# A one-token decode block on one core: the loads move from SyncE's queue to GpSimd's, one packet for each engine's share

## The chip, the cores and the metric

One core of a Trainium2 chip runs the kernel. The metric is the device time of one execution in microseconds (us). Three runs of the kernel before gave 1275.4, 1275.68 and 1275.88 us, a median of 1275.68 us.

## What is computed

The reference, cut to what matters. The key and value caches are bf16 and hold 8 heads of 65536 rows of 256 elements: 268 MB each, read once. Everything else is small.

```
B, Sq, D = 1, 1, 448;  Hq, Hkv, Sk, Dh = 16, 8, 65536, 256
xn = layernorm(A_x)
q = (xn @ A_wq) as 16 heads of 256
scores = q . k_cache * 256**-0.5          # two query heads share a key head
o = softmax(scores) . v_cache             # per head
attn = o.reshape(1, 4096) @ A_wo
g = silu(xn @ B_w_gate); u = xn @ B_w_up; y = (g * u) @ B_w_down
ffn = xn + y * sigmoid(xn @ B_w_r)
out = A_x + attn + ffn
```

## The kernel before

**Tiling.** The 65536 rows of a head are spread over 128 partitions, 512 rows to a partition. A load is a quarter of a head: 128 rows of 512 bytes on each partition, so 64 KB in one piece from each partition, 8192 KB in all. There are 32 such loads of keys (K0 to K31 here) and 32 of values (V0 to V31). In the code U is 4 (quarters), NU is 32, NT is 28, so V28 is `("v", NT)` and V31 is `("v", NT + 3)`. SBUF has three slots of one load each (`ring`): even K in the first, odd K in the second, V0 to V27 in the third. K0 to K4 are loaded in two halves of 4096 KB each, and V31 in five parts of 64, 32, 16, 8 and 8 rows.

**Engines.** For a K load, TensorE transposes the keys (`ps_t`), VectorE and ScalarE copy them out of PSUM (`kt_all`), TensorE multiplies them with the query (`ps_q`), and the scores are gathered in `S_sb`. After four K loads of a head comes the softmax's exponential, and then its four V loads go through `ps_o`. All matrix products of TensorE are recorded under one line, L413; all DMA issues under L914.

**Queues.** Each engine's instructions are put into a list (`prog`) by Python and emitted in that order; a wait at the head of a list holds all that stands behind it. `item` (L241) puts waits and DMA issues on SyncE's list (SP). The order is: `k_first` (the first 16 of the 64 rows of K0's first half, 1024 KB, L288), `wq` (the query's weights, 3584 KB, into the third slot, L289), the rest of K0's first half, K0's second half, K1's halves, then K2 and K3 and V0 and so on, each with a wait for its slot: `FREE` (a K load is transposed), `FREEH` (its first half is), `VFREE` (a V load is multiplied). Near the end stand V28, then the weights `wg` (gate and up, two DMAs), `wd` (down, and x again), `wo` (most of the output weights, 2912 KB), then V29, V30, and V31, which waits for `SUM`, then `wx` and `wo_end` (the rest of the output weights). The last DMA, the output, is on SyncE's list too.

**The other DMAs.** ScalarE's queue issues four small ones: x and w_r at the start (`w0`, L387), and two hops near the end (`hop`, L678). Hop 0 writes `o_row`, the attention output of the first seven heads, 14 rows of 512 bytes, to `o_flat` in HBM; hop 1, which waits for hop 0, reads it back as `oT_h`, 56 bytes on each of 128 partitions. In `ending` (L801) TensorE's order is: V28, the feed-forward products, `ATTN` (L682, the products of `oT_h` with `wo`), then V29, V30, V31. VectorE adds up `SUM` (L828 to L833) after `ATTN`. V31's slot holds `wo`, `oT_h` is read by `ATTN`, and so V31 waits for `SUM`.

**GpSimd** runs `pool_setup` (L315: constants) at the start and nothing afterwards. VectorE's setup begins with a wait for one of these (`z_m1p`, L348), and its layer norm waits for both loads of `w0` (L355).

Of the kernel before, what the change touches and what calls it, by code (L numbers as in the profile page):

```python
# [23 lines left out]
def bass_parallel_sum__gqa_block_cached__moe_arch_mod__decode_kernel(  # L24
# [149 lines left out]
    sems = {}  # L174
# [20 lines left out]
    prog = {e: [] for e in engines}  # L195
    here = [("S", 0)]
# [7 lines left out]
    def put(e, kind, key, fn, sem):  # L204
        if ghost[0] and e == "pe":
            prog[e].append(("g" + kind, lab(e), key, fn, sem))
        elif not ghost[0]:
            prog[e].append((kind, lab(e), key, fn, sem))

    def W(e, *key):  # L210
        put(e, "w", key, None, None)
# [3 lines left out]
    def O(e, key, fn, sem=None, n=1):  # L215
        key = key if isinstance(key, tuple) else (key,)
        if not ghost[0]:
            weight[key] = n
        put(e, "o", key, fn, sem or e)

    def alias(e, *key, sem=None):
        put(e, "a", key, None, sem or e)
# [15 lines left out]
    semtot = {}  # L238
    fed = {}

    def item(key, parts, need=()):  # L241
        for n in need:
            W("sp", *n)
        for ap, src, sem in parts:
            semtot[sem] = semtot.get(sem, 0) + 16
            items[key] = (sem, semtot[sem])
            prog["sp"].append(("d", here[0], ("DMA", key, len(prog["sp"])), (ap, src), sem))

    def rows_src(kd, u, o, J):
        src = A_k_cache if kd == "k" else A_v_cache  # L250
# [64 lines left out]
    def pool_setup():  # L315
        v = nc.gpsimd
        O("pool", "z_identf", lambda it: v.memset(ident_f[:, :], 0.0))
        O("pool", "ones", lambda it: v.memset(ones_f[:, :], 1.0))
        O("pool", "z_sel", lambda it: v.memset(sel_bf[:, :, :], 0.0))
        O("pool", "z_sel2", lambda it: v.memset(sel2_bf[:, :, :], 0.0))  # L320
        O("pool", "z_m1p", lambda it: v.memset(m1p[:, :, :], 0.0))
        O("pool", "z_zero", lambda it: v.memset(zero_bf[:, :], 0.0))
        W("pool", "z_identf")
        O("pool", "identf", lambda it: v.affine_select(
            out=ident_f[:, :], in_=ident_f[:, :], compare_op=ALU.not_equal, fill=1.0,
            base=0, pattern=[[-1, P]], channel_multiplier=1))
        W("pool", "identf")
        O("pool", "identbf", lambda it: v.tensor_copy(out=ident_bf[:, :], in_=ident_f[:, :]))
        W("pool", "identbf")
        for m in range(NG):  # L330
            for i in range(rep):
                O("pool", ("sel", m, i), lambda it, m=m, i=i: v.tensor_copy(
                    out=sel_bf[:, m, i:i + 1], in_=ident_bf[:, 32 * m + i:32 * m + i + 1]))
        for g in range(NG):
            for i in range(rep):
                for n2 in range(2):
                    if g > 0:
                        W("pool", "sel2", g - 1, i, n2)
                    r = 32 * g + n2 * rep + i
                    O("pool", ("sel2", g, i, n2), lambda it, r=r, i=i, n2=n2: v.tensor_tensor(  # L340
                        out=sel2_bf[:, n2, i:i + 1], in0=sel2_bf[:, n2, i:i + 1], in1=ident_bf[:, r:r + 1], op=ALU.add))
        alias("pool", "CONST")
        O("pool", "z_q", lambda it: v.memset(q_cur[:, :, :], 0.0))
        O("pool", "KZ", lambda it: v.memset(kt_all[:, :], 0.0))

    def dve_setup():
        v = nc.vector
        W("dve", "z_m1p")  # L348
        O("dve", "XEZ", lambda it: v.memset(xe_row[:, :, :, :], 0.0), "sc")
        O("dve", "PSQ_ZERO", lambda it: v.memset(ps_q[:, :], 0.0), "ev0")  # L350
        O("dve", "PSO_ZERO", lambda it: v.memset(ps_o[:, :], 0.0), "ev1")
        O("dve", "s2z0", lambda it: v.memset(s2[0][:, :], 0.0), "ev2")
        O("dve", "pssz", lambda it: v.memset(ps_s[:, :], 0.0))
        O("dve", "S2Z", lambda it: v.memset(s2[1][:, :], 0.0))
        W("dve", "DMA", "w0")  # L355
        O("dve", "xf", lambda it: v.tensor_copy(out=x_f, in_=x_row))
        W("dve", "xf")
        O("dve", "mean", lambda it: v.tensor_reduce(out=stat[0:1, 0:1], in_=x_f, axis=AX.X, op=ALU.add))
        W("dve", "mean")
        O("dve", "negmean", lambda it: v.tensor_scalar(out=stat[0:1, 7:8], in0=stat[0:1, 0:1], scalar1=-1.0 / D, scalar2=None,  # L360
                                                       op0=ALU.mult))
        W("dve", "negmean")
        O("dve", "xc", lambda it: v.tensor_scalar(out=xc_f, in0=x_f, scalar1=stat[0:1, 7:8], scalar2=None, op0=ALU.add))
        W("dve", "xc")
        O("dve", "sumsq", lambda it: v.tensor_tensor_reduce(out=xn_f, in0=xc_f, in1=xc_f, scale=1.0, scalar=0.0,
                                                            op0=ALU.mult, op1=ALU.add, accum_out=stat[0:1, 1:2]))
        W("dve", "sumsq")
        O("dve", "VPE", lambda it: v.tensor_scalar(out=stat[0:1, 2:3], in0=stat[0:1, 1:2], scalar1=1.0 / D, scalar2=EPS,
                                                   op0=ALU.mult, op1=ALU.add))
        W("dve", "SQRT")  # L370
        O("dve", "rstd", lambda it: v.reciprocal(out=stat[0:1, 4:5], in_=stat[0:1, 3:4]))
        W("dve", "rstd")
        O("dve", "xn", lambda it: v.tensor_scalar(out=xn_f, in0=xc_f, scalar1=stat[0:1, 4:5], scalar2=None, op0=ALU.mult))
        W("dve", "xn")
        O("dve", "XNBF", lambda it: v.tensor_copy(out=xn_bf, in_=xn_f))
        W("dve", "XNBF")
        W("dve", "XEZ")
        xv = xn_bf.rearrange("o (u s) -> o u s", s=RP)
        for t in range(2):
            e_ = xe_row[0:1, t, :, :].rearrange("o r (u t) -> o r u t", t=2)[:, :, :, t]  # L380
            O("dve", ("xe", t), lambda it, e_=e_, t=t: v.tensor_copy(
                out=e_, in_=xv[:, :, t * (NE - 1):t * (NE - 1) + NE].rearrange("o u r -> o r u")))
        alias("dve", "XE")
        O("dve", "R", lambda it: v.tensor_tensor_reduce(out=x_f, in0=xn_bf, in1=wr_row, scale=1.0, scalar=0.0,
                                                        op0=ALU.mult, op1=ALU.add, accum_out=stat[0:1, 5:6]))

    def act_setup():  # L387
        a = nc.scalar
        for k, (d, s) in enumerate([(x_row, A_x[0]), (wr_row, B_w_r.rearrange("(o n) -> o n", o=1))]):
            prog["act"].append(("d", here[0], ("w0", k), (d, s), "w0"))  # L390
        items["w0"] = ("w0", 32)
        W("act", "VPE")
        O("act", "SQRT", lambda it: a.activation(out=stat[0:1, 3:4], in_=stat[0:1, 2:3], func=ACTF.Sqrt), "evq")
        W("act", "R")
        O("act", "SIG", lambda it: a.activation(out=stat[0:1, 6:7], in_=stat[0:1, 5:6], func=ACTF.Sigmoid), "ev3")
        W("dve", "XNT")
        x = ps_m[0:P, C_XNT:C_XNT + 2 * NE].rearrange("p (t r) -> p r t", t=2)
        y = xnT_sb[:, 0:2 * NE].rearrange("p (r t) -> p r t", t=2)
        z = xnT_sb[:, 2 * NE:4 * NE - 2].rearrange("p (r t) -> p r t", t=2)
        O("dve", "xnt0", lambda it: nc.vector.tensor_copy(out=y, in_=x), "exp")  # L400
        O("dve", "xnt1", lambda it: nc.vector.tensor_copy(out=z[:, :, 0], in_=x[:, 1:NE, 1]))
        O("dve", "XNTSB", lambda it: nc.vector.tensor_copy(out=z[:, :, 1], in_=x[:, 0:NE - 1, 0]))
        W("dve", "QT")
        O("dve", "QTSB", lambda it: nc.vector.tensor_scalar(
            out=qT_sb[:, :, :], in0=ps_m[0:P, C_Q:C_Q + NH * Hq].rearrange("p (q f) -> p f q", f=NH), scalar1=inv_sqrt_dh, scalar2=None, op0=ALU.mult), "pc", 2)
        W("act", "QTSB")
        W("act", "S2Z")
# [393 lines left out]
    def ending():  # L801
# [66 lines left out]
        W("sp", "RESULT", 1)  # L868
        prog["sp"].append(("d", here[0], ("OUT", 0), (out[0], res_bf), "out"))

    pool_setup()
    dve_setup()
    act_setup()
    pe_setup()
# [23 lines left out]
    def emit(e, tail=False):  # L898
        eng = engines[e]
        waited = {}  # L900
        pool = []
# [8 lines left out]
        def do(kind, key, fn, sem, it):  # L910
            if kind == "o":
                fn(it).then_inc(sems[sem], weight[key])
            elif kind == "d":
                eng.dma_start(fn[0], fn[1]).then_inc(sems[sem], 16)  # L914

        def fit(vals, execs, inner):

# [165 lines left out]
        while k < len(entries):  # L1083
            kind, lab, key, fn, sem = entries[k]
# [60 lines left out]
```

## Time and profile before

| | |
|---|---|
| median of three runs | 1275.68 us |
| profiled execution, its own time | 1275.51 us |
| its span, first to last instruction | 1274.2 us |
| TensorE busy | 75% |
| VectorE, ScalarE, GpSimd busy | 45%, 34%, 1% |
| read from HBM | 549 MB, 431 GB/s over the span |

The profiled execution's time is 1.3 us above its span. It is within 0.2 us of the median. Busy shares are shares of the span; a DMA engine counts as busy while one of its packets is in work, and there are 16 such engines.

### The profile page before, as it was taken

The page shows a single profiled execution, that of the slowest core. Times are in us where ns is not written, and L with a number is a line of the kernel's source. Part 1 is how long each engine was busy: PE and PEld are TensorE (multiplying, and loading weights), DVE is VectorE, ACT ScalarE, POOL GpSimd, SP SyncE. Part 2 cuts the span into 40 slices and gives each one's busy share as a digit, 9 for nine tenths or more (in the row PEclk, how much of TensorE's full clock was granted, in tenths as well). Part 3 has the DMA queues.
Part 4 walks back from the last instruction along what each step waited for, and adds up shares of the span by engine and source line. Part 5 has one row for each costly group of instructions (what it writes and reads, how often), then busy time and mean ns, then how long its engine had stood idle before and what let it go on. Part 6 is the DMA issues. An engine that isn't in the chain of part 4 may idle for free.

```text
span 1274.2 us, 23495 instructions
## 1 busy us (share of the span) xinstructions
PE 957.2 (75%) x9729; PEld 624.0 (49%) x9729; DVE 572.1 (45%) x1078; ACT 436.9 (34%) x656; POOL 8.0 (1%) x38
## 2 busy tenths in 40 slices
PE   3899977778777679777778776787777687777854
PEld 3676554445544455444455444454444554444411
DVE  4666544345444455343454444453444544444310
ACT  2455433244332434223333243343333333323300
POOL 2000000000000000000000000000000000000000
PEclk9999988899888899887898888898888988888887
DMA  9999999999999999999999999999999999999998
GB/s 409 427 434 433 441 428 432 438 428 438 436 428 432 438 428 442 432 430 430 438 428 444 430 430 430 438 428 446 428 430 430 438 428 446 428 430 432 430 432 370
DMA packets 12273, 549.22 MB, mean 431 GB/s; under 512 B 1490, under 2 KB 2020, under 8 KB 2532
## 3 DMA queue, kind: packets, MB, share of 16 engines
q1 hardware_dynamic: 12084, 549.03, 99.8%
q8 instruction: 8, 0.13, 0.0%
q10 hardware_dynamic: 176, 0.02, 0.0%
q14 instruction: 5, 0.04, 0.0%
HBM read 549.04 MB, written 0.01 MB: 431 GB/s over the span
## 4 chain that ended last, share of the span: by engine, by line
DMA 76%; PE 19%; ACT 2%; issue 1%; DVE 1%; SPq 0%; ACTq 0%; DVEq 0%
DMA ring<-in_A_v_cache_dram 68%; PE ps_o L413 13%; DMA ring<-in_A_k_cache_dram 4%; PE ps_t L413 4%; DMA kt_all<-in_A_wo_dram 3%; PE ps_q L413 2%; ACT kt_all L474 2%; PE ps_m L413 1%; DVE kt_all L472 0%; ACT S_sb L555 0%; SPq L914 0%; PE ps_s L413 0%; DVE kt_all L718 0%; DVE m1p L525 0%; DVE S_sb L523 0%
## 5 line engine op out<-in xcount | busy, mean ns | idle before, releaser
L413 PE MATMUL ps_t<-ident_f,ring 128*128 128x128 f32 x4096 | 585.0, 284 | 78.1 <-DMA ring<-in_A_k_cache_dram 53.3
L472 DVE COPY kt_all<-ps_t 128x1024 bf16<-128x1024 bf16 x768 | 487.0, 685 | 285.4 <-PE ps_q L413 281.1
L413 PEld LDWEIGHTS ps_t<-ident_f,ring 128*128 128x128 f32 x4096 | 449.4, 143 | 230.0 <-issue 136.4
L474 ACT ACTIVATE kt_all<-ps_t 128x1024 bf16<-128x1024 bf16 x256 | 262.2, 1024 | 500.5 <-PE ps_q L413 500.4
L413 PE MATMUL ps_o<-ring,p_sb 128*4 128x512 bf16 x2044 | 180.7, 517 | 214.0 <-DMA ring<-in_A_v_cache_dram 209.6
L413 PEld LDWEIGHTS ps_o<-ring,p_sb 128*4 128x4 bf16 x2044 | 53.7, 103 | 303.8 <-issue 278.2
L413 PE MATMUL ps_q<-kt_all,q_cur 128*2 128x512 bf16 x2056 | 164.3, 396 | 0.4 <-DVE kt_all L472 0.3
L496 ACT ACTIVATE s<-ps_q 98x512 bf16<-98x512 f32 x257 | 151.8, 591 | 1.3 <-PE ps_q L413 1.3
L578 DVE RECIPROCAL rs<-ps_m 128x4 f32<-128x4 f32 x29 | 5.3, 183 | 279.0 <-PE ps_m L413 279.0
L565 ACT ACTIVATE p_sb<-S_sb 128x128 bf16<-128x128 bf16 x64 | 18.9, 307 | 282.4 <-PE ps_o L413 282.1
L413 PEld LDWEIGHTS ps_s<-sel_bf,s 128*128 128x128 bf16 x1032 | 64.5, 98 | 4.7 <-ACT s L496 1.3
L634 DVE CAST ob_sb<-ps_o 100x512 bf16<-100x512 f32 x29 | 20.1, 692 | 99.2 <-PE ps_o L413 99.2
L413 PE MATMUL ps_s<-sel_bf,s 128*128 128x8 bf16 x1032 | 63.6, 167 | 1.0 <-ACT s L496 1.0
L413 PEld LDWEIGHTS ps_q<-kt_all,q_cur 128*2 128x2 bf16 x2056 | 26.4, 79 | 44.0 <-issue 44.0
L413 PEld LDWEIGHTS ps_m<-rowsum,ones_f 128*128 128x128 f32 x58 | 12.5, 269 | 23.6 <-issue 23.6
L474 ACT ACT_TABLE_LOAD x7 | 9.0, 1283 | 20.6 <-PE ps_q L413 20.6
L525 DVE TENSOR_REDUCE m1p<-S_sb (+1 forms) x33 | 13.9, 422 | 4.4
L413 PE MATMUL ps_m<-rowsum,ones_f 128*128 128x4 f32 x58 | 15.1, 330 | 0.0
L555 ACT ACTIVATE S_sb<-S_sb,negmax 128x512 bf16<-128x512 bf16 x16 | 13.2, 852 | 3.3 <-DVE negmax L549 3.3
L413 PE MATMUL ps_m<-diag,ones_f 2*128 2x2 f32 x58 | 11.2, 260 | 3.8 <-DVE diag L540 0.8
L413 PEld LDWEIGHTS ps_m<-diag,ones_f 2*128 2x128 f32 x58 | 8.7, 187 | 10.6 <-DVE diag L540 10.6
L523 DVE CAST S_sb<-ps_s 128x256 f32 (+1 forms) x33 | 13.7, 415 | 0.1
(96 smaller groups left out, 130.1 us busy)
## 6 DMA issues: line engine op xcount, KB each, us to landing
ring<-in_A_k_cache_dram SPq DMA_DIRECT2D x9, 4096.0 KB, 30.3
ring<-in_A_v_cache_dram SPq DMA_DIRECT2D x1, 4096.0 KB, 35.5
ring<-in_A_wq_dram SPq DMA_DIRECT2D x1, 3584.0 KB, 12.8
ring<-in_A_k_cache_dram SPq DMA_DIRECT2D x1, 3072.0 KB, 21.1
ring<-in_A_wo_dram SPq DMA_DIRECT2D x1, 2912.0 KB, 29.3
ring<-in_A_v_cache_dram SPq DMA_DIRECT2D x1, 2048.0 KB, 39.6
ring<-in_B_w_gate_dram SPq DMA_DIRECT2D x1, 1568.0 KB, 16.4
ring<-in_B_w_up_dram SPq DMA_DIRECT2D x1, 1568.0 KB, 19.8
```

Source lines behind the costliest of these rows:

```text
L413: return pe.matmul(*a, **k)
L472: O(e, ("EV", s, m), lambda it: nc.vector.tensor_copy(out=kt[:, :], in_=tb[:, :]), f"ev{m}")
L474: O(e, ("EV", s, m), lambda it: nc.scalar.activation(out=kt[:, :], in_=tb[:, :], func=ACTF.Copy), f"ev{m}")
L496: O("act", ("EVQ", s), lambda it: nc.scalar.activation(out=s2[s % 2][0:QROWS, :], in_=ps_q[0:QROWS, :], func=ACTF.Copy), "evq")
L523: O("dve", ("SCOPY", u), lambda it: nc.vector.tensor_copy(out=S_sb[:, at(it, SBN), :], in_=ps_sn), "sc")
L525: O("dve", ("SMAX", u), lambda it: nc.vector.tensor_reduce(out=m1p[:, :, at(it, 1)], in_=S_sb[:, at(it, SBN), :].rearrange("p n i -> p i n ...
L555: O("act", ("EXP", h, i), lambda it, i=i: nc.scalar.activation(out=S_sb[:, :, i], in_=S_sb[:, :, i], func=ACTF.Exp, bias=negmax[:, i:i + 1 ...
L565: O("act", ("PC", t, c), lambda it: nc.scalar.activation(out=p_sb[:, c, :, :], in_=S_sb[:, n:n + CH, :], func=ACTF.Copy), "pc")
L578: O("dve", ("RS", t), lambda it: nc.vector.reciprocal(out=rs[:, :, :], in_=ps_m[0:P, C_TOT:C_TOT + NH * rep]))
L634: O("dve", ("OB", t), lambda it: nc.vector.tensor_copy(out=ob_sb[0:OROWS, :], in_=ps_o[0:OROWS, :]))
```

## The change

`item` puts its waits and its DMAs on GpSimd's list instead of SyncE's. `soft` is a switch that is always on, so this holds for every load that `item` makes; the output's DMA stays on SyncE, the four small ones on ScalarE. The loads ahead of the first wait (`k_first`, `wq`, the rest of K0, K1: six DMAs) are emitted ahead of `pool_setup`, all others behind it. A DMA that GpSimd issues carries `single_packet`, which makes each DMA engine's share of the load one packet. The order of the loads, their sizes, their waits and their slots are the same.

```
+    soft = [True]
+
     def item(key, parts, need=()):
+        by = "pool" if soft[0] else "sp"
         for n in need:
-            W("sp", *n)
+            W(by, *n)
         for ap, src, sem in parts:
             semtot[sem] = semtot.get(sem, 0) + 16
             items[key] = (sem, semtot[sem])
-            prog["sp"].append(("d", here[0], ("DMA", key, len(prog["sp"])), (ap, src), sem))
+            prog[by].append(("d", here[0], ("DMA", key, len(prog[by])), (ap, src), sem))
...
+    loads = list(prog["pool"])
+    free = [en[0] for en in loads].index("w")
+    prog["pool"][:] = loads[:free]
     pool_setup()
+    prog["pool"].extend(loads[free:])
     dve_setup()
...
             elif kind == "d":
-                eng.dma_start(fn[0], fn[1]).then_inc(sems[sem], 16)
+                more = {"single_packet": True} if e == "pool" else {}
+                eng.dma_start(fn[0], fn[1], **more).then_inc(sems[sem], 16)
```

## Rows read from the trace of the kernel before

**Rows 1.** The page's span and its line on DMA packets.

```profile
span 1274.2 us, 23495 instructions
DMA packets 12273, 549.22 MB, mean 431 GB/s; under 512 B 1490, under 2 KB 2020, under 8 KB 2532
```

**Rows 2.** One stretch: time, busy PE, PEld, DVE, ACT, POOL, clock, DMA share, GB/s.

```profile
206.99:1135.79 928.80, 703.69 (x7128) 461.25 (x7128) 419.75 (x792) 323.94 (x486) 0.00 (x0) 0.89 1.00 434
```

**Rows 3.** The chain that ended last, 207 to 250 us: start, length, what.

```profile
206.99 3.58 PE ps_o L413 x32
...
212.77 32.80 DMA ring<-in_A_v_cache_dram
245.70 3.58 PE ps_o L413 x32
```

**Rows 4.** The chain's last DMA.

```profile
1228.12 43.53 DMA kt_all<-in_A_wo_dram
```

**Rows 5.** DMA queues: packets, MB, share of 16 engines' span.

```profile
q1 hardware_dynamic: 12084, 549.03, 99.8%
q8 instruction: 8, 0.13, 0.0%
q10 hardware_dynamic: 176, 0.02, 0.0%
```

**Rows 6.** DMA issues: count, KB each, median us from issue to landing.

```profile
ring<-in_A_wo_dram SPq DMA_DIRECT2D x1, 2912.0 KB, 29.3
...
ring<-in_B_w_gate_dram SPq DMA_DIRECT2D x1, 1568.0 KB, 16.4
ring<-in_B_w_up_dram SPq DMA_DIRECT2D x1, 1568.0 KB, 19.8
...
ring<-in_A_k_cache_dram SPq DMA_DIRECT2D x1, 1024.0 KB, 4.8
...
oT_h<-o_flat ACTq DMA_DIRECT2D x1, 7.0 KB, 12.4
```

**Rows 7.** Timeline near the end, SyncE's and ScalarE's issues: start, length.

```profile
1181.13 0.33 SPq L914 DMA_DIRECT2D ring<-in_B_w_gate_dram  x1
1181.50 0.43 SPq L914 DMA_DIRECT2D ring<-in_B_w_up_dram  x1
...
1182.87 0.34 SPq L914 DMA_DIRECT2D ring<-in_A_wo_dram  x1
...
1195.06 0.34 ACTq L914 DMA_DIRECT2D o_flat<-kt_all  x1
...
1199.92 0.36 ACTq L914 DMA_DIRECT2D oT_h<-o_flat  x1
```

**Rows 8.** Timeline of the start: k_first's issue, VectorE's setup, TensorE's first K load.

```profile
0.74 0.39 SPq L914 DMA_DIRECT2D ring<-in_A_k_cache_dram  x1
...
1.35 0.48 DVE L349 MEMSET ring<- 1x512 uint32 x1 [1.35 <-POOL zero_bf L322]
...
5.69 3.27 DVE L356 CAST ring<-ring 1x448 f32<-1x448 bf16 x1 [1.50 <-DMA ring<-in_B_w_r_dram]
...
17.45 0.19 DVE L404 TENSOR_SCALAR qT_sb<-ps_m 128x32 bf16<-128x32 f32 x1 [3.62 <-PE ps_m L413]
...
22.75 1.97 PE L413 MATMUL ps_t<-ident_f,ring 128*128 128x128 f32 x8 [5.41 <-DMA ring<-in_A_k_cache_dram]
```

**Rows 9.** Timeline of the end: ATTN, SUM, and TensorE's wait for V30.

```profile
1217.83 5.08 PE L413 MATMUL ps_q<-ring,oT_h 128*1 128x448 bf16 x26
...
1224.47 0.61 DVE L833 TENSOR_TENSOR kt_all<-ps_q,kt_all 1x448 f32<-1x448 f32 x1
...
1250.99 5.55 PE L413 MATMUL ps_o<-ring,p_sb 128*4 128x512 bf16 x64 [13.74 <-DMA ring<-in_A_v_cache_dram]
```

**Rows 10.** The chain between K0 and K1.

```profile
46.83 2.91 issue
```

**Rows 11.** SyncE's timeline, the issues of K3's halves.

```profile
62.23 11.75 SPq L914 DMA_DIRECT2D ring<-in_A_k_cache_dram  x2
```

## The prediction

> **What bounds the kernel now.** I read the page's line on DMA first, then the wide windows, the chain, and last the two ends. The page has 549 MB at a mean of 431 GB/s over 1274.2 us [rows 1]. From 207 to 1136 us the 16 DMA engines are busy all the time at 434 GB/s while TensorE works 704 of 929 us [rows 2], so no engine limits this stretch. In the chain the pattern is the same for each V load: 5.8 us of TensorE, then 32.8 us from the next V load's issue to its landing [rows 3]. A V load follows the last after 38.71 us (206.99 to 245.70) in which one K and one V load pass, 16.78 MB, so 433.5 GB/s; one load's own passage is half, 19.35 us. So of the 32.8 us some 13.4 are waiting behind the other load: the queue is never dry. The kernel ends shortly after its last weights land (1228.12 + 43.53 = 1271.65, with a span of 1274.2) [rows 1, 4]. A change of the queue can then do three things: change the 433.5 GB/s, let the engines run dry somewhere, or shift the first byte.
>
> The sum is made against the profiled execution's 1275.5 us (span 1274.2 and 1.3 around it), 0.2 below the median of the three runs.
>
> **Fewer packets.** SyncE's queue has 12084 packets [rows 5]. It issues 85 DMAs, and each of 16 engines ends each with a flag, so 12084/16 - 85 = 670 data packets on an engine, one for each partition's piece. As one packet for a share, 85 remain, 585 fewer. Their price: gate and up have 1568 KB each in pieces of 12.25 KB, and land at 1181.13 + 16.4 = 1197.53 and 1181.50 + 19.8 = 1201.30 [rows 6, 7], 3.77 us apart, where 433.5 GB/s gives 3.70. Both have eight packets to an engine, where the same bytes in 64 KB pieces would have 1.5. So about 10 ns a packet, but the landings are rounded, so 0 to 25 ns. Merging may leave a part of it with each descriptor. I take 4.5 us off, from 0 to 9. One sentence on a page: the Trainium skill, DMA: Bandwidth & Descriptors, section on where 436 GB/s comes from, puts the ceiling at 435.2, and by it at most 4.9 us (an estimate, 0.39% of 1266 us) could come off.
>
> **First byte.** SyncE's first load of 1024 KB lands 4.8 us after its issue at 0.74, at 5.54 [rows 6, 8]; its bytes take 2.4, so 2.4 is fixed. No row shows a GpSimd DMA. I bound its surplus by 0 and 1.5 us and take 0.7; it is paid once, because later loads have 13.4 us in front of them.
>
> **GpSimd's setup behind six issues.** VectorE starts at 1.35 when GpSimd has cleared a tile [rows 8]. Six issues, 0.33 to 0.43 each on SyncE [rows 7], are 2.3 us; at 1 us each they would be 6. The query is ready at 17.64 and TensorE starts on K0 only at 22.75, held by the load [rows 8]. This 5.1 us is the cover; VectorE would wait until 5.69 for w_r anyway. Cost: nothing, up to 1 us.
>
> **What shares the engines with the loads.** This is the term that I think decides. ScalarE's hops and the instruction fetches are on other queues (176 and 8 packets) [rows 5] and have to take turns with the loads. How, the hops show. Hop 0 has 14 pieces of 512 bytes, so one packet and one flag to an engine. It is issued at 1195.06, and hop 1, which waits for it, at 1199.92 [rows 7]: at most 4.9 us, though gate, up, down and wo, issued long before it, land only from 1197.5 to 1182.87 + 29.3 = 1212.2 [rows 6, 7]. So it passed between their pieces. Hop 1 has 128 pieces, eight and a flag to an engine, nine turns, and takes 12.4 us [rows 6]: seven more turns, 7.5 us more, 1.07 a turn, where one piece of wo (22.75 KB) takes 0.86. So a turn costs about one packet of the other queue, and 2.8 us are fixed.
>
> With the change a packet is a whole share: 3.7 us for gate, up or down, 6.9 for wo, 19.35 for a V load. Hop 0 arrives at about 1197.8, when up's share has begun. Its data goes at 1201.3, its flag after down at 1205.0. Hop 1 is issued at 1205.1, arrives near 1207.9, and gets its first turn after wo (1212.2), its second after V29 (1231.6), its third after V30 (1251.0, where TensorE's wait for V30 ends [rows 9]; V29 one passage of 19.35 earlier). Now GpSimd's queue is empty, since V31 waits for SUM, and SUM for ATTN, which needs hop 1. The other six turns are free: it lands near 1252. From ATTN's start to SUM's end are 7.25 us (1217.83 to 1225.08) [rows 9], so V31 is issued at 1259.3, and its bytes start with the fixed 2.4. In the same counting the engines would have gone on at 1251.0: 10.7 us without a load. Before, V31 was issued at 1225.1, 25.9 us ahead. Two turns more or fewer change nothing, since all that are left at 1251 are free. V31, wx and the ends follow as before, so the end moves by 10.7 (8.7 to 12.7 with the first byte's bounds and the hop's rest). What was hidden by 25.9 us of cover is late next.
>
> The Trainium skill (DMA: Bandwidth & Descriptors, section on queues, rings and completion order) says that an engine drains a whole packet of one ring before it turns to another; the 1.07 us a turn agrees with it, but no row here has a packet larger than one piece.
>
> **The same at the start.** w_r is such a DMA: VectorE waits for it until 5.69 [rows 8]. If it arrives after k_first's share has begun, its data waits for that share and its flag for wq's (3584 KB, 8.5 us), and lands near 14.7 (5.54 + 0.7 + 8.5); the setup from 5.69 to 17.64 then ends at 26.6, and TensorE starts 3.2 us late (26.6 against 22.75 + 0.7). If it arrives before, 0. Between K0 and K1 TensorE stands 2.91 us with nothing to wait for [rows 10]; I take this as code being fetched on the instruction queue. Such a fetch would wait for the rest of a half load's share, 0 to 9.7 us, 4.8 in the middle. What of that counts: K3's second half is issued when K1 is transposed, at 73.65 (62.23 + 11.75 - 0.33) [rows 11]. Ahead of it are 32256 KB; counted from k_first's landing at 5.54, 31232 KB at 433.5 GB/s end at 79.3, so it must be issued by 76.9. The cover is 3.2 us. TensorE late by 1.6 + 4.8 = 6.4 costs 3.2; I take 3, from 0 to 9.7.
>
> **Sum.** 1275.5 - 4.5 + 0.7 + 10.7 + 3 = 1285.4, say 1285. Its own range: 1279 to 1294; the ends of all terms at once are not to be expected.
>
> **A rule against the change, and what it would make.** VectorE copies PSUM to SBUF for 420 of 929 us [rows 2]. The Trainium skill (SBUF — State Buffer, box on the DVE blocking DMA) warns that some VectorE modes lock GpSimd out while it writes descriptors, and advises SP's or ACT's queue. As a mechanism of this kernel: a load's descriptors may be written late by up to the 13.4 us that it waits in the queue [rows 3] at no cost; only beyond that the engines run dry, and each us counts for every one of some 60 loads.
>
> **Rivals.**
> - The engines still take turns piece by piece, or the hops get through (0.22): for it, hop 1 passed nine times between pieces in 12.4 us, and a flag on the packet's last piece need not change who is served; against it, a turn there costs one packet. Then 1275.5 - 4.5 + 0.7 = 1271.7, faster. It decides at 1251: where hop 1 lands by 1241 (7.25 and 2.4 before V30's end), no engine is dry. Its range is 1268 to 1275.
> - Only the queue changes, the packets stay as they are (0.16): 1275.5 + 0.7 = 1276.2, no change that can be told.
> - GpSimd's descriptors arrive late or some engines fall behind with them (0.06): for it, that no row shows such a load; against it, the 13.4 us of cover. 1% of rate is 12.6 us, so 1288 and up.
> - The forecast, held hops and fetches (0.56): 1285.
>
> **How the numbers follow.** A measurement of this kernel can tell about 0.2%, 2.6 us. Faster (under 1273.1): most of the first rival, 0.19, and 0.01 of the second. Within 0.2%: the rest of these, and 0.01 of the forecast's low end, together 0.19. Slower: 0.61. Cases of both signs hold chance, so the range reaches down into the first rival: 1271 to 1294 leaves out about 0.08 below and 0.09 above.
>
> **What would show it.** If right: the hop's landing grows from 12.4 to over 40 us; SUM ends near 1255 to 1260 instead of 1225; a DMA share clearly under 1 for some 10 us ahead of V31; the packets pass a little faster than 434 GB/s from 207 to 1136. The start right or wrong: VectorE's wait for w_r beyond 5.69, TensorE's first transpose beyond 23.5, a longer gap between K0 and K1, a dry stretch near 77. Wrong: hop 1 back in under 25 us, or TensorE waiting for V loads with the engines idle all along.

## The result, and the profile after

The changed kernel took 1289.41 us, the median of three runs (1286.45 to 1290.52), against 1275.68 before: a ratio of 1.0103 with a 95% interval of 1.0076 to 1.0130. The profiled execution is the shortest of the three, 1286.45 us with a span of 1285.1, so 10.9 us above the profiled execution of before on both counts.

The direction and the range of the prediction hold, and its time, 1285, is close. Its deciding step is wrong all the same: the hops near the end were not held up at all. What costs the time is a step that the prediction does not contain.

First what did not change. The page of the changed kernel, its span, packets and queues, and then the same window as in [rows 2]:

```profile
span 1285.1 us, 23495 instructions
...
DMA packets 11951, 549.22 MB, mean 427 GB/s; under 512 B 1521, under 2 KB 1538, under 8 KB 2210
...
q0 software_dynamic: 11760, 549.03, 98.9%
```

```profile
206.99:1135.79 928.80, 702.15 (x7128) 460.34 (x7128) 419.70 (x792) 323.58 (x486) 25.31 (x48) 0.90 1.00 434
```

GpSimd's queue carries the loads in 11760 packets where SyncE's had 12084 [rows 5]. What went are packets under 8 KB alone (2210 for 2532 [rows 1]), and the trace has 7424 packets of 64 KB in both kernels: the large loads are still in pieces, one for each partition. That the flag makes each engine's share one packet, as the change was described, shows nowhere. The rate is the same 434 GB/s. Now the hops, by the landings of the page and the timeline near the end (start, length, engine, what); the last line is V31's issue before:

```profile
oT_h<-o_flat ACTq DMA_DIRECT2D x1, 7.0 KB, 12.4
```

```profile
1195.99 0.34 ACTq L922 DMA_DIRECT2D o_flat<-kt_all  x1
...
1200.89 0.36 ACTq L922 DMA_DIRECT2D oT_h<-o_flat  x1
...
1218.72 5.08 PE L416 MATMUL ps_q<-ring,oT_h 128*1 128x448 bf16 x26
...
1226.28 2.60 POOL L922 DMA_DIRECT2D ring<-in_A_v_cache_dram  x5 [19.00 <-DVE kt_all L836]
```

```profile
1225.11 2.49 SPq L914 DMA_DIRECT2D ring<-in_A_v_cache_dram  x5
```

Hop 1 lands 12.4 us after its issue, to the tenth as before [rows 6]; `ATTN` starts 0.9 us later than before (1218.72 for 1217.83 [rows 9]), and V31 is issued 1.2 us later (1226.28 for 1225.11). Up to here the change costs about 1 us.

**The join.** One piece of the code was not described above. Each engine's list is cut in two, and only the part ahead of the cut lies in a block. At the end of the block all engines wait for one another; then each emits its tail.

```
            O("pe", ("PV", t, c, k), f)
            if t == NT + 3 and k == 0:
                for e in ("pe", "dve", "act", "pool", "sp"):
                    prog[e].append(("cut", here[0], (), None, None))
...
    with nc.Block() as block:
        block.gpsimd(lambda eng: emit("pool"))
...
    for e in engines:
        emit(e, True)
```

The cut stands behind V31's first part on TensorE. By then all loads have been issued, so it lies at the end of the loads' list whichever engine carries them. A DRAIN is what each engine records at the block's line ahead of the join; POOLq and SPq are the sequencers of GpSimd and SyncE, PEq that of TensorE. The instructions of the block's line (L1099 before, L1107 after), with a count, the shortest, median and longest duration in ns, and the first and last start, are first those of before and then those of after:

```profile
L1099 POOLq DRAIN  x1: 4064/4064/4064, 4.7 to 4.7; - x1
...
L1099 SPq DRAIN  x1: 124/124/124, 1253.9 to 1253.9; - x1
```

```profile
L1107 POOLq DRAIN  x1: 46806/46806/46806, 1229.8 to 1229.8; - x1
```

Before, SyncE drained in 0.12 us at 1253.9, with weights under way that landed up to 1271.65 [rows 4]. After, GpSimd's drain begins at 1229.8, as it issues its last loads, and lasts 46.8 us, to 1276.6. TensorE's timeline at this place, with the idle time before a group and its releaser in brackets, before and after; the last line of each is the output's DMA:

```profile
1260.71 2.60 PE L413 MATMUL ps_o<-ring,p_sb 128*4 128x512 bf16 x32 [4.17 <-DMA ring<-in_A_v_cache_dram]
1263.63 1.99 PE L413 MATMUL ps_t<-ring,p_sb 128*4 128x512 bf16 x5 [0.33 <-PEq L1099]
...
1273.05 0.26 SPq L914 DMA_DIRECT2D out_dram<-kt_all  x1
```

```profile
1261.64 2.68 PE L416 MATMUL ps_o<-ring,p_sb 128*4 128x512 bf16 x32 [4.20 <-DMA ring<-in_A_v_cache_dram]
...
1276.92 1.44 PE L416 MATMUL ps_t<-ring,p_sb 128*4 128x512 bf16 x3 [12.60 <-PEq L1107]
...
1283.59 0.36 ACT L868 ACTIVATE kt_all<-ps_s 1x240 bf16<-1x240 f32 x1 [25.79 <-PE ps_s L416]
...
1283.98 0.31 SPq L922 DMA_DIRECT2D out_dram<-kt_all  x1
```

TensorE stands 12.6 us at the join instead of 0.33. V31's other parts land meanwhile, but the work on them, which before ran beside the last landings, starts only at 1276.92.

The output's DMA is issued at 1283.98 instead of 1273.05, 10.9 us later: the last landing 0.8 later (1272.44, read in the run with the join at the end, for 1271.65); from it to the end of the drain 4.2; release of TensorE 0.3; and from there to the output 7.06, where before only 1.40 lay between the last landing and the output, so 5.7. 0.8 + 4.2 + 0.3 + 5.7 = 11.0, within rounding the whole difference between the two profiled executions. The median of the changed kernel lies 3.0 us higher still; two causes of its spread are shown with the last experiment.

### The profile page after: what moved, and what is told of

The parts are those of the page before. It is cut to its first block, busy times and chain, and to the rows that moved or that the text cites. A ratio compares the mean times of both kernels' runs of the same rounds, so it can differ in the third digit from the quotient of the medians.

```text
span 1285.1 us, 23495 instructions
## 1 busy us (share of the span) xinstructions
PE 954.4 (74%) x9729; PEld 622.6 (48%) x9729; DVE 574.4 (45%) x1078; ACT 436.5 (34%) x656; POOL 56.6 (4%) x122
## 2 busy tenths in 40 slices
DMA packets 11951, 549.22 MB, mean 427 GB/s; under 512 B 1521, under 2 KB 1538, under 8 KB 2210
## 3 DMA queue, kind: packets, MB, share of 16 engines
q0 software_dynamic: 11760, 549.03, 98.9%
## 5 line engine op out<-in xcount | busy, mean ns | idle before, releaser
L922 POOL DMA_DIRECT2D ring<-in_A_v_cache_dram x36 | 19.0, 528 | 766.7 <-PE ps_o L416 715.9
L922 POOL DMA_DIRECT2D ring<-in_A_k_cache_dram x38 | 20.2, 533 | 379.3 <-PE ps_t L416 378.5
```

The costliest lines, as they stand in the source:

```text
L922: eng.dma_start(fn[0], fn[1], **more).then_inc(sems[sem], 16)
```

## The experiments

Three theories stood against one another. A: the join waits for GpSimd's drain, which ends only some us after the landing of GpSimd's own loads. B: the packet flag holds up other traffic (a fetch of code at the end among it). C: GpSimd's queue is slower as such. Each run is beside the kernel before on the same chip.

**The last loads on SyncE's queue.** V31, wx and wo_end go back to SyncE.

```
...
+    soft[0] = False
-    slot_item("v", NT + 3, 2, [("last%d" % k if k < len(LAST) - 1 else "slot2", J) for k, J in enumerate(LAST)], [("SUM",)])
+    slot_item("v", NT + 3, 2, [("last%d" % k, J) for k, J in enumerate(LAST)], [("SUM",)])
```

> The changed kernel, but V31, wx and wo_end are issued by SyncE again (V31's last part counts on a semaphore of its own). Theory A (the join): all engines join once, after V31's first part, and GpSimd comes to the join only when its drain is over, which lasts until its own DMAs have landed and some 4 us more. Here GpSimd's last load is V30, which lands near 1252, so its drain is over near 1256, before TensorE arrives at 1264: TensorE's wait at the join goes from 12.6 us to under 1, and the time to 1276.4 us (1275.9 to 1277.2), the 0.9 us that the first load starts later being left. Theory B (packets): large packets hold TensorE's code fetch near the end; the last loads are no such packets here, so also about 1276. Theory C (GpSimd's queue is slower as such): 54 of its loads are still there, 1284 or more.

Measured: 1279.1 us (1278.1 to 1280.39), ratio 1.0027 [1.0017, 1.0037]. The block's line and TensorE's timeline in this run:

```profile
L1108 POOLq DRAIN  x1: 59997/59997/59997, 1206.0 to 1206.0; - x1
...
L1108 SPq DRAIN  x1: 121/121/121, 1229.5 to 1229.5; - x1
```

```profile
1263.06 7.92 PE L417 MATMUL ps_o<-ring,p_sb 128*4 128x512 bf16 x96 [20.78 <-DMA ring<-in_A_v_cache_dram]
...
1271.34 0.81 PE L417 MATMUL ps_t<-ring,p_sb 128*4 128x512 bf16 x3 [0.35 <-PEq L1108]
```

SyncE drains in 0.12 us with nine loads under way; GpSimd's drain ends at 1266.0, 3.6 us after the last packet of V30, its last load (1262.4), and TensorE waits 0.35 us at the join. So A holds, but 2.7 us stand above the time that A gave. They are in the second fence: V30 lands near 1263 instead of 1251 [rows 9]. The two queues took turns (from 1227 to 1260 the trace has 167 packets on GpSimd's and 162 on SyncE's), V31's parts on SyncE's overtook V30 on GpSimd's, and the products of V30 and V31 came in one row at the end.

**Without the packet flag.** `more` is empty, everything else as in the changed kernel.

```
-                more = {"single_packet": True} if e == "pool" else {}
+                more = {}
```

> The changed kernel without the packet flag: all loads still on GpSimd's queue. Theory A (the join waits for GpSimd's drain): no change against the changed kernel, 1286 to 1291 us, TensorE waits 12 to 16 us at the join, GpSimd's drain ends near 1276 to 1280. Theory B (a share as one packet holds the code fetch of TensorE at the end): the hold is gone, about 1276 us. If the flag makes packets cheaper, the passage from 207 to 1136 us is slower here than 434 GB/s by up to 0.4%.

Measured: 1287.46 us (1286.8 to 1287.93), ratio 1.0092 [1.0076, 1.0107]. Queue and drain:

```profile
q0 software_dynamic: 11760, 549.03, 98.8%
```

```profile
L1107 POOLq DRAIN  x1: 47292/47292/47292, 1229.3 to 1229.3; - x1
```

The loss stays, with the same 11760 packets and the same drain. B falls. The two medians still differed by 2 us, so both kernels were timed again side by side (last in this section).

**The join at the end.** The cut is put behind all work of the tail.

```
-            if t == NT + 3 and k == 0:
-                for e in ("pe", "dve", "act", "pool", "sp"):
-                    prog[e].append(("cut", here[0], (), None, None))
...
     ending()
+    for e in ("pe", "dve", "act", "pool", "sp"):
+        prog[e].append(("cut", here[0], (), None, None))
```

> The changed kernel with the engines' join moved behind all of the work, the output's DMA included. Theory A: TensorE no longer waits in front of V31's last parts, its tail follows the landings as before the change (last products near 1273.5), and only the kernel's end waits for GpSimd's drain, which ends 3 to 4 us after the last landing, near 1276.7: 1278 us (1276.5 to 1280). Theory B: the code fetch near the end is still held until the loads have passed, 1284 to 1290.

Measured: 1278.76 us (1278.64 to 1278.91), ratio 1.0025 [1.0015, 1.0034]. The end of the chain, the output's issue, and the drain:

```profile
1229.42 43.02 DMA kt_all<-in_A_wo_dram
```

```profile
1273.85 0.31 SPq L921 DMA_DIRECT2D out_dram<-kt_all  x1
```

```profile
L1106 POOLq DRAIN  x1: 46654/46654/46654, 1229.8 to 1229.8; - x1
```

The output leaves 0.8 us later than before, so nothing between start and output costs more than that. The last weights land at 1272.44 and the drain ends at 1276.45, 4.0 us behind; with no work left, the kernel ends with it. That is A with its remainder.

**Only the end's weights on GpSimd's queue.** The kernel before, with wx and wo_end moved, waiting for `SUM` (the edit is shown against the changed kernel).

```
-    soft = [True]
+    soft = [False]
...
+    soft[0] = True
-    item("wx", [(wo_x, wo_rows(FR - WX, FR), "wx")], [("HT",)])
+    item("wx", [(wo_x, wo_rows(FR - WX, FR), "wx")], [("SUM",)])
```

> The kernel before, but wx and wo_end alone (0.69 MB of 549) on GpSimd's queue, with the flag, issued when SUM is there. Theory A: GpSimd's drain waits for these DMAs; they have 36 turns on each engine between V30's and V31's pieces (2.42, 1.21 us and less a turn), so they land near 1269.5, the drain is over near 1273, TensorE waits 9 us at the join and ends 6.6 us after it: 1282 us (1278 to 1287). Theory B: shares of 14 KB hold nothing, 1275.7. Theory C: 0.13% of the bytes cannot matter, 1275.7.

Measured: 1276.8 us (1276.59 to 1277.18), ratio 1.0010 [1.0001, 1.0019]; A's 1282 was missed.

```profile
L1108 POOLq DRAIN  x1: 31417/31417/31417, 1227.2 to 1227.2; - x1
```

```profile
kt_all<-in_A_wo_dram POOLq DMA_DIRECT2D x2, 112.0 KB, 29.1
```

In their own queue these few packets passed between V31's pieces, and the last of them ended at 1258.0, not near 1270; so the drain was over at 1258.6, before TensorE came to the join at 1266. The step that failed is the landing; the drain again ended behind it, but here by 0.6 us only. What is left of a loss, 1.3 us, is not the join: TensorE came to it 2.7 us later than before, with V31's first part 1.7 us later (1262.44 for 1260.71). By itself this run does not tell A from C.

**All loads behind V28 on SyncE's queue.** GpSimd still carries 515 of the 549 MB.

```
...
+    soft[0] = False
...
-    slot_item("v", NT + 1, 1, None, [("FREE", NU - 1)])
-    slot_item("v", NT + 2, 0, None, [("VFREE", NT)])
+    slot_item("v", NT + 1, 1, [("fin1", SBN)], [("FREE", NU - 1)])
+    slot_item("v", NT + 2, 0, [("fin2", SBN)], [("VFREE", NT)])
...
```

> The changed kernel, but all loads behind V28 (gate, up, down, wo, V29, V30, V31, wx, wo_end) go back to SyncE's queue; V29, V30 and V31's last part have semaphores of their own. GpSimd still carries 30 of 32 K-and-V pairs less three V loads, 59 loads. Theory A (the join waits for GpSimd's drain, which ends some 4 us after GpSimd's own last landing): that landing is V28's, near 1195 to 1200, the drain is over by 1205, TensorE's wait at the join is under 0.5 us, and what is left is the later first byte, 0.8 us: 1276.3 us (1275.8 to 1277.5). V28 may land some 2 us later than before, since it takes turns with gate, up and down, and has cover. Theory C (GpSimd's queue is slower as such, over the whole span): the loss is nearly that of the changed kernel, 1288 to 1289.

Measured: 1276.49 us (1276.35 to 1277.8), ratio 1.0006 [0.9997, 1.0016].

```profile
q0 software_dynamic: 9792, 515.38, 93.4%
q1 hardware_dynamic: 2292, 33.66, 6.2%
```

```profile
L1110 POOLq DRAIN  x1: 45007/45007/45007, 1155.9 to 1155.9; - x1
```

```profile
1266.98 1.44 PE L419 MATMUL ps_t<-ring,p_sb 128*4 128x512 bf16 x3 [0.34 <-PEq L1110]
```

The drain is over by 1200.9, TensorE waits 0.34 us at the join, and of the loss 0.9 us are left. C falls: a queue that carries 94% of the bytes costs under 1 us when nothing joins behind it.

**The join earlier, in both kernels.** The cut is put behind the first half of V30's products, in the changed kernel and, as the control, in the kernel before.

```
-            if t == NT + 3 and k == 0:
+            if t == NT + 2 and k == 0 and c == 0:
```

> The changed kernel with the join one step earlier, behind the first half of V30's products instead of behind V31's first part. Theory A: the join is released at the same moment, near 1276.9, since that is set by the last landing of GpSimd's loads; TensorE waits some 22 us there (from about 1254.6), and behind it stand, beside the 6.6 us of the changed kernel, the second half of V30's products and V31's first 32, 64 products at 0.055 to 0.086 us, 3.5 to 5.5 us, with one copy of ScalarE between them that may add up to 0.8: 1294 us (1292.5 to 1296). Theory C, or a fixed cost at the end of a kernel with loads on GpSimd's queue: 1289.4, unchanged.

> The kernel before with the same earlier join, as the control to the run with the join behind the first half of V30's products. All loads are on SyncE's queue. Theory A: GpSimd's drain ends at the start of the kernel, nothing at the join waits for a landing, TensorE loses some 0.4 us there beside work that waits for V31's parts anyway: 1275.5 to 1276.3 us. If an earlier join costs time by itself (an engine that comes late to it), 1280 and above.

Measured: 1290.43 us (1289.96 to 1291.14), ratio 1.0114 [1.0098, 1.0131], in the changed kernel; 1275.6 us (1275.45 to 1275.78), ratio 1.0000 [0.9990, 1.0009], in the kernel before. The changed kernel with the early join, and then the control:

```profile
1276.89 6.24 PE L416 MATMUL ps_o<-ring,p_sb 128*4 128x512 bf16 x64 [21.70 <-PEq L1107]
...
1288.67 0.31 SPq L922 DMA_DIRECT2D out_dram<-kt_all  x1
```

```profile
1255.26 2.46 PE L413 MATMUL ps_o<-ring,p_sb 128*4 128x512 bf16 x32 [0.49 <-PEq L1099]
```

The join is left at 1276.89, as at 1276.92 in the changed kernel, though TensorE came to it 9 us earlier: GpSimd sets the moment. The control shows that an early join costs nothing when SyncE carries the loads. The expected 1292.5 to 1296 was missed. It added 3.5 to 6.3 us of work to the median of 1289.4; the medians differ by 1.0 (by 2.2 from the second median of the changed kernel, 1288.23, below). The time behind the join grew from 7.06 to 11.78 us, 4.7, against the first profile of the changed kernel and by 3.2 against the second (8.61 us, below). TensorE's clock is part of this difference, so the moment of the join is firm here and the price of the added work is not.

**The changed kernel and the one without the flag again, side by side.**

> The changed kernel unaltered, timed beside the one without the packet flag on the same chip. The three times of the changed kernel lie between 1286.45 and 1290.52 us, those without the flag between 1286.8 and 1287.9. If the flag does nothing, both have the same median, between 1286.5 and 1289.5, under 1 us apart, and both show the same spread; what spreads is TensorE's clock after its long wait at the join, with some 6.6 to 8 us of work behind it.

> The changed kernel without the packet flag, beside the changed kernel on the same chip. If the flag does nothing: the same median within 1 us, the same packets (11760 on GpSimd's queue), the same hop of 12.4 us. If the flag costs what the two medians so far differ by: 2 us below the changed kernel.

Measured: 1288.23 us (1286.45 to 1289.58), ratio 1.0095 [1.0078, 1.0112], and 1287.82 us (1286.7 to 1291.47), ratio 1.0103 [1.0086, 1.0121]. The medians are 0.4 us apart and either spread is wider than that; without the flag hop 1 lands in 12.2 us. The flag does nothing that these runs can tell. The spread has two sources, which the profiled execution of the changed kernel (1289.58 here) shows:

```profile
54.45 1.07 PE L416 MATMUL ps_t<-ident_f,ring 128*128 128x128 f32 x8 [3.06 <-issue]
...
78.60 0.53 POOL L922 DMA_DIRECT2D ring<-in_A_k_cache_dram  x1 [10.87 <-PE ps_t L416]
...
1278.51 1.44 PE L416 MATMUL ps_t<-ring,p_sb 128*4 128x512 bf16 x3 [12.27 <-PEq L1107]
...
1287.12 0.31 SPq L922 DMA_DIRECT2D out_dram<-kt_all  x1
```

The join is left 1.6 us later than in the first profile, because a stall at the start made K3's second half late (below), and from there to the output are 8.61 us for 7.06. TensorE's granted clock between these two moments is 0.66 here and 0.81 there: it comes out of 12 us of standing at the lower of its two levels (1.2 GHz) in both, and rises to the higher (2.4 GHz) 5.9 us behind the join here and 2.8 there. Three products side by side take 0.59 us at the lower level and 0.39 at the higher one. The kernel without the flag shows this cause alone: its two profiles leave the join at 1276.84 and 1277.00, at a clock of 0.68, and the output follows 8.39 and 8.31 us later. So the clock's part of the expectation is right; the start was not in it.

## Why the prediction was right or wrong

| step | predicted, us | measured, us |
|---|---|---|
| fewer packets | -4.5 | 0 |
| first byte | +0.7 | +0.8 |
| GpSimd's setup behind six issues | 0, up to 1 | TensorE 4.0 late; at the end 0, or 1.5 |
| hops held by whole shares | +10.7 | 0 |
| the same at the start (w_r, code) | +3 | 0 |
| the join behind GpSimd's drain | not seen | +10.2 |
| sum | 1285.4 | 1286.45 (1275.5 + 11.0) |

**Right direction, wrong mechanism.** The two large numbers agree, 10.7 and 10.2, by chance. The sum landed close because an effect that did not happen was as large as one that was not foreseen, and the -4.5 and the +3 that did not come about nearly cancel.

**The step that failed** is "What shares the engines with the loads". It took "each share one packet" at its word and let a turn last a whole share. The hop's 12.4 us, with the flag and without, say that turns still last one piece; the first rival had it so, with a chance of 0.22. The Trainium skill (DMA: Bandwidth & Descriptors, section on queues, rings and completion order) says that an engine drains a whole packet of one ring before it serves the next. If a flagged share were such a packet, hop 1 could not have landed in 12.4 us; so on this kernel either the flag makes no such packet or the packet is not drained whole. The runs do not tell these apart, and no rate hangs on it: 434 GB/s in both.

**Fewer packets** fell with it. The prediction's second rival (only the queue changes, 1276.2) describes the loads best, and 1276.49 with the end on SyncE's queue is its number. What the rival, and the first one, lacked was the price of the join.

**Why the join was missed.** The prediction moved 85 DMAs past GpSimd's list and asked who waits for data or for a slot. It did not ask what else waits for the engine itself. The trace of before had the row: TensorE released by the block's line at 1263.63 after 0.33 us, cheap, and so not asked about. A wait that costs 0.33 us says only that its condition was met early under the old assignment. The rows of the drains would not have settled it. SyncE's 0.12 us at 1253.9, with loads still under way, is a drain that does not wait for loads; GpSimd's 4.06 us end at 8.76 with its last own operation, so they show a drain that waits for the engine's own work:

```profile
5.21 3.51 POOL L344 MEMSET kt_all<- 128x4096 bf16 x1
```

What GpSimd's would do with loads under way no row of before shows, and the bounds would have been 0.3 us and a wait up to the last landing and beyond.

**First byte.** GpSimd issues `k_first` at 1.24 (SyncE: 0.74 [rows 8]), and it lands 5.2 us later for 4.8 [rows 6]: 0.9 later, and 0.8 at the last landing. Right.

```profile
1.24 0.68 POOL L922 DMA_DIRECT2D ring<-in_A_k_cache_dram  x1 [0.80 <-SPq L1107]
```

```profile
ring<-in_A_k_cache_dram POOLq DMA_DIRECT2D x1, 1024.0 KB, 5.2
```

**The setup.** The start of the changed kernel (start, length, engine, what, idle before):

```profile
5.17 0.48 DVE L352 MEMSET ring<- 1x512 uint32 x1 [5.17 <-POOL zero_bf L325]
...
6.75 6.24 POOL L343 TENSOR_TENSOR sel_bf<-sel_bf,ring 128x1 bf16<-128x1 bf16 x16
...
7.93 0.32 DVE L359 CAST ring<-ring 1x448 f32<-1x448 bf16 x1
...
9.10 3.84 DVE L366 TENSOR_SCALAR ring<-ring,stat 1x448 f32<-1x448 f32 x1
...
12.96 3.50 POOL L347 MEMSET kt_all<- 128x4096 bf16 x1
...
14.23 2.48 DVE L376 TENSOR_SCALAR ring<-ring,stat 1x448 f32<-1x448 f32 x1
...
21.93 0.19 DVE L407 TENSOR_SCALAR qT_sb<-ps_m 128x32 bf16<-128x32 f32 x1 [3.39 <-PE ps_m L416]
...
26.70 1.94 PE L416 MATMUL ps_t<-ident_f,ring 128*128 128x128 f32 x8 [4.88 <-issue]
```

VectorE starts 3.8 us later and the query is ready 4.5 us later than before [rows 8]. The prediction had 5.1 us of cover here, between the query and the landing of K0. That was misread: behind its last product for the query, at 21.82 (26.70 - 4.88), TensorE stands 4.88 us in which it waits for nothing that the profile shows. Before, that product ended at 17.34 (22.75 - 5.41 [rows 8]), and 17.34 + 4.88 = 22.22 lies 0.5 us ahead of the load at 22.75: of the 5.1 us some 0.5 were cover, and the rest hid this standing. TensorE starts K0 4.0 us later, the query's 4.5 less the 0.5.

w_r was not held: the cast that needs it starts at 7.93 without a wait. As to code, the trace has a packet of 16 KB on the instruction queue that starts at 24.00, 2.70 us ahead of TensorE's start on K0. In all eight profiles with the first loads on GpSimd's queue this distance is 2.70 to 2.77 us, so the standing ends with a fetch of code.

The stall between K0 and K1 has such a packet too. In the five profiles that show the stall, TensorE goes on 3.65 to 3.69 us behind the packet's start: 46.09 and 49.74 before, 50.76 and 54.45 in the second profile of the changed kernel. In these five the packet starts 23.3 to 24.8 us behind TensorE's start on K0, in the six without the stall 20.2 to 21.6 us. Both ends of the first range come from profiles with the loads on SyncE's queue, so GpSimd's loads did not hold the packet longer. That the stall is code being fetched is thus borne out; why the packet comes late in some executions stays open.

TensorE made up 2.9 of its 4.0 us in the first profile, because the stall of 2.95 us [rows 10] is gone there: K3's second half is issued at 74.72, and the limit of 76.9 plus the 0.8 of the first byte, 77.7, is kept. Where the stall comes on top, as in the second profile (3.06 us at 54.45), the issue is at 78.60, past the limit by 0.9, and V loads are issued 1.5 us later from there on (371.23 for 369.70). So the cover of 3.2 us that the prediction worked out for K3 is right to within 0.6 us. What the start costs at the end, 0 in some executions and 1.5 in others, comes from the setup and the stall, and not from w_r or code held behind whole shares.

**DVE and GpSimd.** Descriptors held up beside VectorE's copies for longer than the 13.4 us that a load waits in the queue would have shown as a rate below 434 GB/s. There is none, with VectorE busy 420 of 929 us; a shorter hold-up these rows do not rule out.

## What to carry to other kernels

When work moves to another engine's list, look not only at who waits for its data but at every place where engines wait for one another: a join that cost 0.3 us with the loads on SyncE cost 12.6 us with them on GpSimd, since GpSimd's drain waits for its own loads. Either the loads near the end go on a queue whose drain does not wait (1276.5 us with all behind V28 moved, 1279.1 with only the last nine, which then overtook V30), or the join goes behind the last work (1278.8). And a wait that hides other waiting is no cover: of 5.1 us of "held by the load" some 0.5 us were slack.

## What the runs showed of the hardware

- GpSimd's drain at the end of a block lasts until its own loads have landed and some time more. In eight profiles it ends 3.3 to 4.0 us behind the end of their last packet (1266.0 behind 1262.4, 1276.45 behind 1272.56), and 0.6 us behind it where only the end's weights were on its queue (1258.6 behind 1258.0). SyncE's takes 0.12 us with loads under way. What the time behind the landing is, and why it differs, is not shown.
- Loads on two queues alternate piece by piece (167 packets on one and 162 on the other in 33 us). That let small loads pass (the end's weights, alone on GpSimd's queue, had landed by 1258.0 where they landed up to 1271.65 behind V31), and it held V30 back by some 12 us where V31 was on the other queue (1263 for 1251).
- A GpSimd issue of a load takes 0.53 us, SyncE's 0.33 to 0.43 [rows 7]; no rate follows from it here.
- VectorE is held up beside GpSimd's long memset at the start. Before, its cast of 448 elements took 3.27 us [rows 8] and ended at 8.96, the memset at 8.72 (5.21 + 3.51, above); after, the cast ran ahead of the memset and took 0.32 us, but a scalar operation on 448 elements beside it took 2.48 us and ended at 16.71, the memset at 16.46. The Trainium skill (SBUF — State Buffer, section on the two separate sides) tells of one pair of ports that the two share, with an exclusive lock that blocks the other for a whole instruction; these two ends agree with it. A third hold-up such a lock does not explain: VectorE's scalar operation at 9.10 took 3.84 us (0.44 before, the line below), and one of GpSimd's sixteen small products beside it 3.75 (0.19 before). Both ended near 12.95, and what held both is not shown.

```profile
9.81 0.44 DVE L363 TENSOR_SCALAR ring<-ring,stat 1x448 f32<-1x448 f32 x1
```
